# Reordering the attention handoffs of a recurrent-memory kernel: where q is turned, where scores start, how tAB is transposed and when vA leaves PSUM

## The chip, the cores and the metric

The kernel runs on one core of one Trainium2 chip. The metric is the device time of one execution in microseconds (us); smaller is better. The kernel before took 2384.8 us (median of three executions, 2383.08 to 2384.88).

## The reference, cut to what matters

Two independent branches read the same x (2048 rows of 1024, bf16) and are mixed by a gate. Branch A is a transformer layer that walks over 64 segments of 32 rows, one after the other: the first 8 rows of a segment's output are the memory rows that stand ahead of the next segment. Branch B is a feed-forward block without any recurrence.

```python
for s in range(n_seg):                      # 64 segments, one after the other
    xs = x[:, s * seg_len:(s + 1) * seg_len, :].copy()
    h = jnp.concatenate([mem, xs], axis=1)  # 8 memory rows + 32 rows
    q = jnp.einsum('btd,dhe->bhte', h, Wq)  # 32 heads of 128
    k = jnp.einsum('btd,dhe->bhte', h, Wk)
    v = jnp.einsum('btd,dhe->bhte', h, Wv)
    scores = jnp.einsum('bhqe,bhke->bhqk', q, k) * scale
    scores = jnp.where(mask[None, None], scores, -1000000000.0)
    p = _softmax(scores, axis=-1)
    o = jnp.einsum('bhqk,bhke->bhqe', p, v)
    o = jnp.einsum('bhte,hed->btd', o, Wo)
    mem = o[:, :M, :].copy()                # needed by the next segment
    outs.append(o[:, M:, :])
...
return g * a + (1 - g) * (_gelu(x @ w_gate) * (x @ w_up) @ w_down)
```

## The kernel before, in words

**Order.** The program is a list of operations, each with an engine, written in one order by hand; every engine runs its own operations strictly in that order, and a small planner (`_Prog`) adds semaphore waits from what each operation reads and writes. Two kinds of waits matter below. A PSUM bank is tracked as a whole: an operation waits for the last operation of every other engine on that bank. SBUF is tracked by address, and many tiles share addresses: `vA` lies on `oT` (and on the stage "o"), `pAB` on `kT`, `E8` and `tAB` on `qT` (which is also the stage "q"), and the stage "p" (`pS` in the profile) on `oRc` and `a_bf`.

**A step** is one segment. Its 32 heads are worked in two halves of 16 ("0" and "1" in the code; the trace's first and second attention of a step). The weights do not fit into SBUF: each of Wq, Wk, Wv, Wo is cut into pieces of 128 x 2048 (512 KB), 8 for each half. 50 slots hold them; 14 of the slots are shared by a piece of either half, so that each step reloads 14 pieces (2 of k, 2 of q, 4 of v, 6 of o) as soon as the first half has used them. A q, k or v piece is 4 matmuls of 512 columns that run beside each other in four column groups. The order of pieces in a step (`HEAD` and `BODY`, L322) is: k0 0-3, q0 0-1, the previous step's o1 4-7, q0 2-3, v0 0-3, k0 4-7, q0 4-7, v0 4-7; then k1, q1, o0 (in four groups of two pieces), v1, and o1 0-3. `on(m, r, n, ...)` in `plan` (L848) hangs other work ahead of the n-th piece of matrix m and half r.

**From projections to attention.** A projection leaves its bank through ScalarE into a stage (`evac`, L614), TensorE turns it by four 128 x 128 transposes (`turn`, L631) and VectorE copies it out (`trans`, L617). `scores` (L644) does the mask and score matmuls into bank SS, then VectorE and ScalarE do the softmax, up to a 128 x 512 32-block transpose into `tAB` (L672). `attend` (L674) multiplies by `vA` (L681) and by `vB` (L686, the second 256 columns of `tAB`) into the banks B0, B1, B2 and SS; `take` copies the four banks into `oT`; `rest_o` (GpSimd, L702) saves eight columns.

**Around the change.** In a step s > 0 the first half's q is turned ahead of v0's piece 6 through bank TT, its scores run ahead of k1's piece 0, `vA` is evicted (ScalarE) ahead of q1's piece 3, which is after k1's eviction into `pS` (ahead of q1's piece 1); the attention runs ahead of o0. Then k1 and q1 are turned through TT, and the second half's scores run ahead of o0's last group (6).

**Step boundary.** The output sum of two halves sits in bank XO; `fold(s, 0)` (VectorE, L763 and L764) adds its first half into `a_bf`, `next_mem` (L773, L776) turns it into the next step's memory columns, and k0 of the next step can begin. TensorE does f2's pieces or `warm` (L799) matmuls meanwhile. `fold(s, 1)` follows ahead of q0's piece 2, and a GpSimd DMA (L938) saves `a_bf` to `a_scr`.

**Fills.** The memory-free part of the projections (the last 8 rows of each segment) is made for four segments at a time (`fill`, L789): one or two such units a step up to step 58, `FILL` (L832): (k,1) and (q,1) when s % 4 is 0; (v,0) and (q,0) when 1; (v,1) when 2; (k,0) when 3. The first unit is evicted by `fill_evac` into the stage "k", and if it is k or q it is turned (`fill_put`, L816: TensorE, VectorE L821, and a GpSimd DMA into `qk_scr`, L824) ahead of o1's piece 2. The second (always q) is put out of the stage "o" ahead of the next step's v0 piece 2.

After the 64 steps come the remaining output rows (L960) and branch B (from L971), which the change does not touch.

Of the kernel before, what the change touches and what calls it, by code (L numbers as in the profile page):

```python
# [191 lines left out]
class _V:  # L192
# [11 lines left out]
    r = _T.r  # L204
# [6 lines left out]
def bass_gated_mix__memory_aug_recurrent_mem_tr__geglu_ffn__prompt_kernel(  # L211
# [34 lines left out]
    with ExitStack() as es:  # L246
# [380 lines left out]

        def turn(st):
            def f(e):
                for j in range(4):  # L630
                    ins = e.transpose(PBV[TT][:, j * 128:(j + 1) * 128], st[:, j * 128:(j + 1) * 128], ident[:, :])  # L631
                return ins
            op("pe", f, rd=[st.r(), ident.r()], wr=[BK(TT)])

        def trans(to, st):
            turn(stage[st])
            dve_copy(to[:, :, :, 0:32].rearrange("p j g c -> p (j g) c"),
                     PBV[TT][:, 0:512].rearrange("p (j g c) -> p (j g) c", g=4, c=32), [BK(TT)], [to.r()])

# [4 lines left out]
        def scores(u):  # L644

            def f(e):
# [24 lines left out]
               rd=[E8.r(), st8.r(8, 16)], wr=[pAB.r(256)])  # L671
            op("dve", lambda e: e.transpose(tAB[:, :], pAB[:, 0:512]), rd=[pAB.r()], wr=[tAB.r()], after=[fin])  # L672

        def attend(u, by=((2, "act"), (3, "dve"), (0, "act"), (1, "dve"))):  # L674
            bo = (B0, B1, B2, SS)

            def f(e):
                for j in range(4):
                    for g in range(4):
                        r = slice(32 * g, 32 * g + 32)  # L680
                        e.matmul(PB[bo[g]][:, j * LQ:(j + 1) * LQ], lhsT=vA[r, j, :],  # L681
                                 rhs=tAB[r, 64 * j:64 * j + LQ],
                                 start=(j == 0), stop=False, skip_group_check=True)
                for g in range(4):
                    r = slice(32 * g, 32 * g + 32)
                    ins = e.matmul(PB[bo[g]][:, 0:4 * LQ].rearrange("p (j c) -> p j c", j=4)[:, :, 24:40], lhsT=vB[r, u, :],  # L686
                                   rhs=tAB[r, 256:512].rearrange("p (j x) -> p j x", j=4)[:, :, 24:40],
                                   start=False, stop=True, skip_group_check=True)
                return ins
            op("pe", f, rd=[vA.r(), tAB.r(), vB.r()], wr=[BK(b) for b in bo])  # L690
            take(by)
            if len(by) == 4:
                rest_o(u)

        def take(by):
            n = 4 * LQ
            for g, eng in by:
                b = (B0, B1, B2, SS)[g]
                cp[eng](oT[:, g, :, :].rearrange("p j c -> p (j c)"), PB[b][:, 0:n], [BK(b)], [oT.r(g * n, (g + 1) * n)])
# [115 lines left out]

        def fill_put(m, u, G, st):  # L816
            if m == "v":
                return
            st = stage[st]
            turn(st)  # L820
            op("dve", lambda e: e.tensor_copy(st[:, :].rearrange("p (i x c) -> p x i c", i=4, x=16),  # L821
                                              PBV[TT][:, 0:512].rearrange("p (x i c) -> p x i c", x=16, i=4)), rd=[BK(TT)], wr=[st.r()])
            m4 = 3 * u if m == "q" else 1 + u
# [16 lines left out]
        def some(fs, n):  # L840
            return lambda: run(fs, n)
# [6 lines left out]
        def plan(s):  # L848
# [37 lines left out]
            on("v", 0, 4, lambda: put_rest())  # L886
            on("v", 0, 6, lambda: trans(qT, "q"))
            if s == 0:
                on("k", 1, 0, lambda: load_v(0, slice(0, 1)))
            on(*(("k", 1, 1) if s == 0 else ("q", 1, 3)), lambda: evac(bank_of["v", 0], vA, "act"))  # L890
            on("k", 1, 1 if s == 0 else 0, lambda: scores(ua))
            if s == 0:
                on("k", 1, 1, lambda: attend(ua))
                on("k", 1, 1, lambda: fill0("k", 1, B0, "k"))
# [6 lines left out]
            if s > 0:  # L901
                on("o", 0, 0, lambda: attend(ua, ((0, "dve"), (1, "dve"))))
            on("o", 0, 0, lambda: trans(kT, "p" if s else "k"))
            on("o", 0, 0, lambda: put_rest())
            on("o", 0, 0, lambda: evac(bank_of["q", 1], stage["q"], "act"))
            if s > 0:
                on("o", 0, 0, lambda: take(((2, "dve"), (3, "dve"))))
                on("o", 0, 0, lambda: rest_o(ua))
            on("o", 0, 2, lambda: trans(qT, "q"))
            on("o", 0, 6, lambda: scores(ub))  # L910
            on("v", 1, 0, some(f1, 3))
# [4 lines left out]
            if fl:  # L916
                on("o", 1, 0, lambda: fill_evac(*fl[0], A1, "k"))
                on("o", 1, 2, lambda: fill_put(*fl[0], "k"))
            if not last:
# [7 lines left out]
            nx = dict(s=s + 1)  # L927
            on("k", 0, 0, lambda: fold(s, 0), **nx)
            on("k", 0, 0, some(f2, 4) if two else lambda: warm(5), **nx)
            on("k", 0, 0, lambda: next_mem(s, 0), **nx)  # L930
            on("k", 0, 0, some(f2, 4) if two else lambda: warm(2), **nx)
            if two:
# [175 lines left out]
```

## Time and profile before

| | |
|---|---|
| median of three executions | 2384.8 us (2383.08 to 2384.88) |
| the profiled execution's own time | 2371.4 us |
| its span, first to last instruction | 2369.6 us |
| granted TensorE clock, mean | 0.983 |
| the 64 steps, first to last `fold(s, 0)` | 121.8 to 1724.3 us |
| mean step, 50 steps from 446.9 to 1697.0 us | 25.0 us |
| busy: TensorE matmul, VectorE, ScalarE, GpSimd | 2130.4, 1044.7, 519.1, 432.9 us |

The profile is one execution. Engines are PE (TensorE matmul), PEld (its weight loads), DVE (VectorE), ACT (ScalarE), POOL (GpSimd) and SP (SyncE, which issues most DMAs). L617 is line 617 of the kernel. In a timeline row stand the start in us, the time, the engine, the line, the operation, output<-inputs, how many were merged, and in brackets how long the engine had idled and what ended that. In the rows of the waits stand: engine, line, who was waited for, then us in total, number of times, the longest. A profiled execution is 13.4 us shorter than the median of the others, so a difference worked out from it is put on the median.

### The profile page before, as it was taken

Reading aid. Unit: us, or ns where it says so; the run is one execution under the profiler, and the core shown is the slowest. Engines: PE = TensorE matmul, PEld = TensorE weight load, DVE = VectorE, ACT = ScalarE, POOL = GpSimd, SP = SyncE. Lnnn points to the kernel's source line nnn. Section 1 sums busy time; section 2 is a strip of 40 time slices with the busy share of each in tenths; the row PEclk is TensorE's granted clock in tenths of the full one; section 3 lists DMA queues with packets and bytes.
Section 4 is the critical chain, followed back from the end, with each engine's and each line's share of the span. In section 5 each row is a group of like instructions: output and inputs, shape, how many; then the busy total and the mean of one; then the engine's idle time right before and its main releaser. Section 6 shows DMA issues by size and latency. Waiting matters only on the chain.

```text
span 2369.6 us, 74769 instructions
## 1 busy us (share of the span) xinstructions
PE 2130.4 (90%) x33827; PEld 1054.9 (45%) x33852; DVE 1044.7 (44%) x2438; ACT 519.1 (22%) x985; POOL 432.9 (18%) x821
## 2 busy tenths in 40 slices
PE   4588888989999998999899989988899999999999
PEld 2244444444444444444444444444464444444444
DVE  3344444444444444444444444444415436264463
ACT  1122222222222222222222222222103213032130
POOL 4322222222222222212222222222100000000000
PEclk9799999999999999999999999999999999999999
DMA  9979999989999999999899989999976260713530
GB/s 374 349 267 315 326 321 329 333 309 320 322 316 322 319 323 314 324 324 322 307 321 326 312 318 326 323 318 330 336 249 200 76 217 10 249 53 101 174 99 18
DMA packets 261453, 639.42 MB, mean 270 GB/s; under 512 B 28264, under 2 KB 102760, under 8 KB 261136
## 3 DMA queue, kind: packets, MB, share of 16 engines
q1 hardware_dynamic: 237312, 597.66, 72.4%
q0 software_dynamic: 13888, 26.31, 3.5%
q10 hardware_dynamic: 9936, 10.69, 1.3%
q8 instruction: 266, 4.36, 0.7%
q14 instruction: 51, 0.42, 0.0%
HBM read 596.85 MB, written 37.68 MB: 268 GB/s over the span
## 4 chain that ended last, share of the span: by engine, by line
PE 48%; DMA 29%; DVE 8%; issue 7%; ACT 5%; POOL 3%; ACTq 0%; SPq 0%; POOLq 0%
DMA a_scr<-a_bf 16%; PE pb L1009 14%; DMA wall<-wo_scr 6%; PE pb L719 6%; PE pb L1063 6%; PE pb L735 5%; PE pb L752 3%; PE pb L789 3%; DMA wall<-in_A_Wo_dram 2%; PE pb L960 2%; PE pb L1044 2%; PE pb L631 2%; PE pb L799 2%; ACT pS L614 1%; DMA xr_scr<-xr 1%
## 5 line engine op out<-in xcount | busy, mean ns | idle before, releaser
L719 PE MATMUL pb<-sl,hT 128*32 128x512 bf16 x12288 | 770.1, 382 | 7.2 <-issue 5.0
L719 PEld LDWEIGHTS pb<-sl,hT 128*32 128x32 bf16 x12288 | 342.4, 97 | 273.7 <-DVE hT L776 21.7
L789 PE MATMUL pb<-sl,hR 128*32 128x512 bf16 x3072 | 224.0, 393 | 9.2 <-issue 8.3
L1009 PE MATMUL pb<-xT,wg 128*128 128x512 bf16 x896 | 211.7, 379 | 0.7
L1009 PE MATMUL pb<-xT,wu 128*128 128x512 bf16 x896 | 211.7, 379 | 0.0
L752 PE MATMUL pb<-wall,oT 128*32 128x256 bf16 x4048 | 152.1, 276 | 38.0 <-DMA wall<-wo_scr 16.5
L763 DVE COPY part<-pb 64x256 f32<-64x256 f32 x128 | 54.0, 422 | 265.9 <-PE pb L752 263.4
L735 PE MATMUL pb<-wall,oT 128*32 128x512 bf16 x2048 | 153.1, 396 | 7.6 <-issue 0.2
L614 ACT ACTIVATE kS<-pb 128x512 bf16<-128x512 f32 x127 | 75.8, 597 | 367.9 <-PE pb L719 349.2
L617 DVE CAST oT<-pb 128x160 bf16<-128x160 f32 x382 | 105.5, 318 | 110.3 <-PE pb L686 110.3
L702 POOL COPY oRc<-oT 128x128 bf16<-128x128 bf16 x128 | 96.2, 752 | 313.3 <-DVE oT L617 311.9
L661 ACT ACTIVATE E<-pb 128x320 bf16<-128x320 f32 x128 | 56.0, 437 | 428.1 <-DVE pb L660 428.1
L1063 PE MATMUL pb<-wd,GT 128*128 128x512 bf16 x657 | 144.9, 379 | 2.1 <-DMA wd<-in_B_w_down_dram 1.2
L752 PEld LDWEIGHTS pb<-wall,oT 128*32 128x32 bf16 x4048 | 97.7, 97 | 93.8 <-issue 36.8
L1009 PEld LDWEIGHTS pb<-xT,wg 128*128 128x128 bf16 x896 | 87.0, 98 | 108.1 <-DVE GT L1025 3.7
L1017 ACT ACTIVATE s<-pb 128x512 f32<-128x512 f32 x112 | 66.7, 596 | 311.6 <-PE pb L1009 311.6
L1009 PEld LDWEIGHTS pb<-xT,wu 128*128 128x128 bf16 x896 | 87.5, 98 | 105.9
L1018 DVE SCALAR_TENSOR_TENSOR tp<-s,pb 128x512 f32<-128x512 f32 x112 | 77.0, 687 | 124.1 <-ACT s L1017 123.9
L659 DVE TENSOR_REDUCE st<-pb 128x8 f32<-128x320 f32 x128 | 62.9, 492 | 137.5 <-PE pb L653 137.5
L617 DVE COPY kT<-pb 128x512 bf16<-128x512 bf16 x128 | 53.7, 420 | 156.6 <-PE pb L631 156.6
L828 POOL COPY kT<-qkr 128x128 bf16<-128x128 bf16 x128 | 37.3, 291 | 451.6 <-DVE kT L617 389.3
L789 PEld LDWEIGHTS pb<-sl,hR 128*32 128x32 bf16 x3072 | 84.7, 99 | 68.6 <-issue 20.9
(93 smaller groups left out, 2249.9 us busy)
## 6 DMA issues: line engine op xcount, KB each, us to landing
wall<-wo_scr SPq DMA_DIRECT2D x336, 512.0 KB, 6.9
sl<-in_A_Wv_dram SPq DMA_DIRECT2D x268, 512.0 KB, 10.8
sl<-in_A_Wk_dram SPq DMA_DIRECT2D x142, 512.0 KB, 5.7
sl<-in_A_Wq_dram SPq DMA_DIRECT2D x142, 512.0 KB, 8.4
wd<-in_B_w_down_dram SPq DMA_DIRECT2D x42, 1024.0 KB, 5.5
wall<-in_A_Wo_dram SPq DMA_DIRECT2D x52, 512.0 KB, 7.9
wdF<-in_B_w_down_dram SPq DMA_DIRECT2D x7, 1024.0 KB, 7.7
wo_scr<-wall SPq DMA_DIRECT2D x12, 512.0 KB, 11.9
```

Source lines behind the costliest of these rows:

```text
L614: op("act", lambda e: e.activation(o, i, ACTF.Copy), rd=rd, wr=wr)
L617: op("dve", lambda e: e.tensor_copy(o, i), rd=rd, wr=wr)
L659: op("dve", lambda e: e.tensor_reduce(nm, sS, AX.X, ALU.max, negate=True), rd=[BK(SS)], wr=[st8.r(0, 8)])
L702: op("pool", lambda e: e.tensor_copy(oRc[:, :, 16 * u:16 * u + 16].rearrange("p c x -> p x c"), oT[:, :, :, 32:40].rearrange("p g j c -> p ...
L719: ins = e.matmul(PB[bk][32 * g:32 * g + 32, :], lhsT=h[:, i, :], rhs=w[:, g * 512:(g + 1) * 512], start=(n == 0), stop=(n == 7))
L735: ins = e.matmul(PB[XO][32 * g:32 * g + 32, :], lhsT=oT[:, j, x, 0:32], rhs=wall[:, na:nb + 1:nb - na, c:c + 256], start=(n == 0 and hp == 0),
L752: ins = e.matmul(PB[XO][32 * g:32 * g + 32, 256 * b:256 * b + 256], lhsT=oT[:, j, x, 0:32], rhs=w[:, c:c + 256], start=False, stop=(n % 4 ...
L789: ins = e.matmul(PB[b][32 * g:32 * g + 32, :], lhsT=h[:, k[2], :], rhs=w[:, g * 512:(g + 1) * 512], start=(n == 0), stop=(n == 7))
L1009: ins = e.matmul(PB[bk][:, 0:FB], lhsT=w[:, kc, cc:cc + 128], rhs=xT[:, :, :, kc, :].rearrange("p t i c -> p (t i) c"), start=(kc == 0), s ...
L1017: op("act", lambda e, hg=hg: e.activation(s1[:, :], hg, ACTF.Square, scale=SQ), rd=[BK(bg)], wr=[s1.r()])
L1018: op("dve", lambda e, hg=hg, t=t: e.scalar_tensor_tensor(out=t[:, :], in0=s1[:, :], scalar=1.0, in1=hg, op0=ALU.add, op1=ALU.mult), rd=[BK ...
L1063: ins = e.matmul(PB[bank[2 * k + hf]][:, :], lhsT=GT[:, j, tb * 128:(tb + 1) * 128], rhs=w[:, jj, hf * 512:(hf + 1) * 512], start=(j == 0) ...
```

## The change

Five edits, for the steps s > 0 unless said otherwise. (1) The first half's q is turned ahead of v0's piece 5 instead of 6, through bank A0 instead of TT, and its scores run ahead of v0's piece 7 instead of k1's piece 0. (2) `vA` of the first half is evicted ahead of k1's piece 4, which in ScalarE's order is now ahead of `pS`; the first attention's fourth bank is A0 instead of SS. (3) Of the first attention's four copies, VectorE does the first and the last and ScalarE the two between; the second half's q is turned through SS; the second half's scores run ahead of o0's group 4 instead of 6 (the title of the change counts pieces: a group is two). (4) `tAB` is transposed in two halves of 256 columns, and `attend` is two operations, the first of which needs the first half only (both attentions, all steps). (5) The first fill is evicted into the stage "q" instead of "k"; if it is k or q, its turn is done through SS right after `fold(s, 0)` at the step boundary, and its VectorE copy and its DMA after `next_mem(s, 0)`, instead of ahead of o1's piece 2.

```diff
--- before.py
+++ after.py
@@ -625,17 +625,17 @@
             else:
                 cp[how](t[:, :], PB[bank][:, :], [BK(bank)], [t.r()])
 
-        def turn(st):
+        def turn(st, bank=TT):
             def f(e):
                 for j in range(4):
-                    ins = e.transpose(PBV[TT][:, j * 128:(j + 1) * 128], st[:, j * 128:(j + 1) * 128], ident[:, :])
+                    ins = e.transpose(PBV[bank][:, j * 128:(j + 1) * 128], st[:, j * 128:(j + 1) * 128], ident[:, :])
                 return ins
-            op("pe", f, rd=[st.r(), ident.r()], wr=[BK(TT)])
-
-        def trans(to, st):
-            turn(stage[st])
+            op("pe", f, rd=[st.r(), ident.r()], wr=[BK(bank)])
+
+        def trans(to, st, bank=TT):
+            turn(stage[st], bank)
             dve_copy(to[:, :, :, 0:32].rearrange("p j g c -> p (j g) c"),
-                     PBV[TT][:, 0:512].rearrange("p (j g c) -> p (j g) c", g=4, c=32), [BK(TT)], [to.r()])
+                     PBV[bank][:, 0:512].rearrange("p (j g c) -> p (j g) c", g=4, c=32), [BK(bank)], [to.r()])
 
         sS = PB[SS][:, 0:320].rearrange("p (a c) -> p a c", a=8)
         nm, sm = st8[:, 0, :], st8[:, 1, :]
@@ -669,33 +669,38 @@
                 in0=E8[:, :, 32:40].rearrange("p (j c) k -> p j c k", c=2),
                 in1=sm.rearrange("p (j c) -> p j c", c=2).unsqueeze(3).to_broadcast([128, 4, 2, 8]), op=ALU.mult),
                rd=[E8.r(), st8.r(8, 16)], wr=[pAB.r(256)])
-            op("dve", lambda e: e.transpose(tAB[:, :], pAB[:, 0:512]), rd=[pAB.r()], wr=[tAB.r()], after=[fin])
-
-        def attend(u, by=((2, "act"), (3, "dve"), (0, "act"), (1, "dve"))):
-            bo = (B0, B1, B2, SS)
+            for c in (0, 256):
+                op("dve", lambda e, c=c: e.transpose(tAB[:, c:c + 256], pAB[:, c:c + 256]), rd=[pAB.r(c, c + 256)], wr=[tAB.r(c, c + 256)], after=[fin])
+
+        def attend(u, by=((2, "act"), (3, "dve"), (0, "act"), (1, "dve")), b3=SS):
+            bo = (B0, B1, B2, b3)
 
             def f(e):
                 for j in range(4):
                     for g in range(4):
                         r = slice(32 * g, 32 * g + 32)
-                        e.matmul(PB[bo[g]][:, j * LQ:(j + 1) * LQ], lhsT=vA[r, j, :],
-                                 rhs=tAB[r, 64 * j:64 * j + LQ],
-                                 start=(j == 0), stop=False, skip_group_check=True)
+                        ins = e.matmul(PB[bo[g]][:, j * LQ:(j + 1) * LQ], lhsT=vA[r, j, :],
+                                       rhs=tAB[r, 64 * j:64 * j + LQ],
+                                       start=(j == 0), stop=False, skip_group_check=True)
+                return ins
+
+            def f2(e):
                 for g in range(4):
                     r = slice(32 * g, 32 * g + 32)
                     ins = e.matmul(PB[bo[g]][:, 0:4 * LQ].rearrange("p (j c) -> p j c", j=4)[:, :, 24:40], lhsT=vB[r, u, :],
                                    rhs=tAB[r, 256:512].rearrange("p (j x) -> p j x", j=4)[:, :, 24:40],
                                    start=False, stop=True, skip_group_check=True)
                 return ins
-            op("pe", f, rd=[vA.r(), tAB.r(), vB.r()], wr=[BK(b) for b in bo])
+            op("pe", f, rd=[vA.r(), tAB.r(0, 256)], wr=[BK(b) for b in bo])
+            op("pe", f2, rd=[tAB.r(256), vB.r()], wr=[BK(b) for b in bo])
             take(by)
             if len(by) == 4:
                 rest_o(u)
 
-        def take(by):
+        def take(by, b3=SS):
             n = 4 * LQ
             for g, eng in by:
-                b = (B0, B1, B2, SS)[g]
+                b = (B0, B1, B2, b3)[g]
                 cp[eng](oT[:, g, :, :].rearrange("p j c -> p (j c)"), PB[b][:, 0:n], [BK(b)], [oT.r(g * n, (g + 1) * n)])
 
         def rest_o(u):
@@ -813,13 +818,19 @@
             else:
                 act_copy(st[:, :], PB[b][:, :], [BK(b)], [st.r()])
 
-        def fill_put(m, u, G, st):
+        def fill_turn(m, st, bank=TT):
+            if m != "v":
+                turn(stage[st], bank)
+
+        def fill_put(m, u, G, st, bank=None):
             if m == "v":
                 return
             st = stage[st]
-            turn(st)
+            if bank is None:
+                bank = TT
+                turn(st)
             op("dve", lambda e: e.tensor_copy(st[:, :].rearrange("p (i x c) -> p x i c", i=4, x=16),
-                                              PBV[TT][:, 0:512].rearrange("p (x i c) -> p x i c", x=16, i=4)), rd=[BK(TT)], wr=[st.r()])
+                                              PBV[bank][:, 0:512].rearrange("p (x i c) -> p x i c", x=16, i=4)), rd=[BK(bank)], wr=[st.r()])
             m4 = 3 * u if m == "q" else 1 + u
             op("pool", lambda e: e.dma_start(qk_scr[:, 4 * G:4 * G + 4, m4, :], st[:, :].rearrange("p (i y) -> p i y", i=4)),
                rd=[st.r()], wr=[("D", "qk", G, m, u)], lane="fq")
@@ -884,12 +895,14 @@
             if s == 0:
                 on("v", 0, 4, lambda: load_qk(0, 0))
             on("v", 0, 4, lambda: put_rest())
-            on("v", 0, 6, lambda: trans(qT, "q"))
+            on("v", 0, 5 if s else 6, lambda: trans(qT, "q", A0 if s else TT))
+            if s > 0:
+                on("v", 0, 7, lambda: scores(ua))
             if s == 0:
                 on("k", 1, 0, lambda: load_v(0, slice(0, 1)))
-            on(*(("k", 1, 1) if s == 0 else ("q", 1, 3)), lambda: evac(bank_of["v", 0], vA, "act"))
-            on("k", 1, 1 if s == 0 else 0, lambda: scores(ua))
+            on("k", 1, 1 if s == 0 else 4, lambda: evac(bank_of["v", 0], vA, "act"))
             if s == 0:
+                on("k", 1, 1, lambda: scores(ua))
                 on("k", 1, 1, lambda: attend(ua))
                 on("k", 1, 1, lambda: fill0("k", 1, B0, "k"))
                 on("q", 1, 0, lambda: fill0("q", 1, B1, "q"))
@@ -899,23 +912,28 @@
                 on("v", 0, 5, lambda: load_qk(s, 1))
             on(*(("q", 1, 1) if s else ("o", 0, 0)), lambda: evac(bank_of["k", 1], stage["p" if s else "k"], "act"))
             if s > 0:
-                on("o", 0, 0, lambda: attend(ua, ((0, "dve"), (1, "dve"))))
-            on("o", 0, 0, lambda: trans(kT, "p" if s else "k"))
-            on("o", 0, 0, lambda: put_rest())
-            on("o", 0, 0, lambda: evac(bank_of["q", 1], stage["q"], "act"))
-            if s > 0:
-                on("o", 0, 0, lambda: take(((2, "dve"), (3, "dve"))))
-                on("o", 0, 0, lambda: rest_o(ua))
-            on("o", 0, 2, lambda: trans(qT, "q"))
-            on("o", 0, 6, lambda: scores(ub))
+                on("o", 0, 0, lambda: attend(ua, ((0, "dve"),), A0))
+                on("o", 0, 0, lambda: evac(bank_of["q", 1], stage["q"], "act"))
+                on("o", 0, 0, lambda: trans(kT, "p"))
+                on("o", 0, 0, lambda: put_rest())
+                on("o", 0, 0, lambda: take(((1, "act"), (2, "act")), A0))
+                on("o", 0, 2, lambda: trans(qT, "q", SS))
+                on("o", 0, 2, lambda: take(((3, "dve"),), A0))
+                on("o", 0, 2, lambda: rest_o(ua))
+                on("o", 0, 4, lambda: scores(ub))
+            else:
+                on("o", 0, 0, lambda: trans(kT, "k"))
+                on("o", 0, 0, lambda: put_rest())
+                on("o", 0, 0, lambda: evac(bank_of["q", 1], stage["q"], "act"))
+                on("o", 0, 2, lambda: trans(qT, "q"))
+                on("o", 0, 6, lambda: scores(ub))
             on("v", 1, 0, some(f1, 3))
             on("o", 1, 0, lambda: evac(bank_of["v", 1], vA, "act"))
             on("o", 1, 0, some(f1, 3))
             on("o", 1, 0, lambda: attend(ub))
             on("o", 1, 0, some(f1, 8))
             if fl:
-                on("o", 1, 0, lambda: fill_evac(*fl[0], A1, "k"))
-                on("o", 1, 2, lambda: fill_put(*fl[0], "k"))
+                on("o", 1, 0, lambda: fill_evac(*fl[0], A1, "q"))
             if not last:
                 on("o", 1, 0, lambda: load_qk(s + 1, 0, "sp"))
             on("o", 1, 0, lambda: op("sp", lambda e: e.dma_start(o_scr[s], oRc[:, :, :].rearrange("p c x -> p (c x)")),
@@ -926,8 +944,12 @@
                 return
             nx = dict(s=s + 1)
             on("k", 0, 0, lambda: fold(s, 0), **nx)
+            if fl:
+                on("k", 0, 0, lambda: fill_turn(fl[0][0], "q", SS), **nx)
             on("k", 0, 0, some(f2, 4) if two else lambda: warm(5), **nx)
             on("k", 0, 0, lambda: next_mem(s, 0), **nx)
+            if fl:
+                on("k", 0, 0, lambda: fill_put(*fl[0], "q", SS), **nx)
             on("k", 0, 0, some(f2, 4) if two else lambda: warm(2), **nx)
             if two:
                 on("q", 0, 2, lambda: fill_evac(*fl[1], B0, "o"), **nx)
```

## The prediction, as it was put on record

> **What bounds the kernel now.** I read the 40 slices first, then the busy table of a stretch in the 64 steps, then the waits, then the timeline of single steps.
>
> ```profile
> DMA  9979999989999999999899989999976260713530
> ```
>
> The 64 steps (121.8 to 1724.3 us) fill slices 2 to 29. There the DMA engines are over 0.9 busy all the time, and so is PE:
>
> ```profile
> 1000.00:1200.00 200.00, 181.23 (x3780) 91.47 (x3773) 91.83 (x246) 44.84 (x89) 48.20 (x97) 1.00 0.91 316
> ```
>
> In 200 us, 181.23 us are PE's and the DMA share is 0.91. Two resources are near their end, and neither is full: what is left is waits in a chain. Summing PE's idle time by the lines on its two sides, over 49 steps, gives 2.3 us of a 25.0 us step: 0.77 ahead of the first attention, 0.30 ahead of the second, 0.36 between Wo pieces of o1 (they wait for their weights), and 0.08 ahead of the fill's turn. The waits name the causes:
>
> ```profile
> ACT pS L614 <- DMA a_scr<-a_bf: 95.4, 61, 3.6
> PEld pb L681 <- ACT vA L614: 129.6, 123, 3.4
> PE pb L681 <- DVE tAB L672: 24.8, 51, 1.7
> ```
>
> `pS` lies on `a_bf`, so in 61 of 63 steps k1's eviction waits until the store of `a_bf` has landed; `vA` stands behind it on ACT, and the first attention behind `vA`. One such step:
>
> ```profile
> 1012.55 0.60 ACT L614 ACTIVATE pS<-pb 128x512 bf16<-128x512 f32 x1 [1.15 <-DMA a_scr<-a_bf]
> 1012.78 0.71 DVE L672 STREAM_TRANSPOSE tAB<-pAB 128x512 bf16<-128x512 bf16 x1
> 1013.04 0.59 ACT L614 ACTIVATE vA<-pb 128x512 bf16<-128x512 f32 x1
> 1013.69 0.27 PE L681 MATMUL pb<-tAB,vA 32*128 32x40 bf16 x16 [0.17 <-ACT vA L614]
> ```
>
> Landing, `pS`, `vA` 0.49 behind it, attention 0.65 behind that. The second attention mostly waits for the whole `tAB`; the fill's turn waits for its eviction:
>
> ```profile
> 1122.77 0.28 PE L681 MATMUL pb<-tAB,vA 32*128 32x40 bf16 x16 [0.36 <-DVE tAB L672]
> ...
> 1124.33 0.40 PE L631 MATMUL pb<-ident,kS 128*128 128x128 bf16 x4 [0.20 <-ACT kS L614]
> ```
>
> **The change, part by part.** Each gain is worked out in 49 steps (447 to 1697 us) from the start and end times in the trace.
>
> *First attention (edits 1, 2, 4).* `vA` moves into the time in which ACT waits for the landing. In steps with s % 4 of 1 and 2 its tile also waits for the store of the stage "o", which mostly lands 0.3 to 0.9 us ahead of `a_scr`; `pS` then slips by 0.15 at most. The new bank A0 makes the attention wait for `pS` itself: 0.65 after its start instead of 1.14 (queued behind on PE: k1's turn and o0). Turning q a piece earlier costs PE nothing as I read it: today its transposes start 0.29 us after ACT's end, and 0.05 behind ACT is possible (a fill's turn); a piece takes 0.21 (64 matmuls in 3.65 us), so they start 0.21 sooner with one piece less ahead of them. Scores and `tAB` come 0.21 sooner, the first half of `tAB` 0.33 more (half of 0.71); the second half 0.05 later than the whole would (an estimate for one more instruction; bounds 0 and 0.2, the shortest DVE rows, and DVE then idles, so either end costs little). With the new start as the latest of q1's last matmul, `pS` + 0.06 and half of `tAB`, and with the `vB` part waiting for the second half, the gain is 0.31 to 0.43 by kind of step, **mean 0.38**.
>
> *Second attention (edits 3, 4).* From the first attention to the second scores it is 2.71 us in 43 of 49 steps, though `qT` is out 0.37 earlier (1015.96 against 1016.39 in the step at 1000 us): o0's group 6 stands between. That goes, and `tAB`'s half gives another 0.33; then `vA`'s eviction after v1 is late next. Gain 0.28. ACT's two copies (0.25 each, behind q's 0.60) end before their Wo groups are due, and the last VectorE copy 0.6 before its own. In 8 or so steps of 49 the `qkr` load for the score's memory columns lands too late to use it all; I take off 0.02: **0.26**.
>
> *Fill's turn (edit 5), in two steps of four.* It takes 0.33 (four transposes) plus the 0.20 wait out of o1 and puts 0.33 behind `fold`. `fold` takes 0.97 to `next_mem`; f2's four pieces cover 0.85 of it, `warm(5)` 1.06. So `next_mem` comes 0.05 later in the one kind and 0.30 in the other. Net (0.48 + 0.23) / 4 = **0.18** a step. VectorE's copy (0.42) and the store move behind `next_mem`, where DVE and POOL idle.
>
> Were PE the only bound: 0.38 + 0.26 + 0.18 = 0.82 a step, 52 us over 63 steps.
>
> *What the DMAs take back.* The third of the six reloaded Wo pieces is what o1's last piece ahead of `fold` needs. In 24 of 47 steps that piece starts 0.13 to 0.14 us after the landing: there the step's end hangs on the DMA and nothing gained between o0 and o1 counts. The Wo reloads begin when o0 has used its pieces, so the first attention's gain moves them, unless the queue is still full: in 22 of 49 steps the first Wo piece lands only 1.41 to 1.47 after the last Wv piece, the closest seen, and moves by nothing. Taking for each step the later of PE's new arrival and the third landing so moved, the 0.82 becomes 0.45, less 0.09 for `next_mem` in the two kinds, and 0.02 for `qkr`: 0.34 a step, **21 us**.
>
> *The new store.* It leaves from the stage "q", which the next step's first q eviction overwrites. The store is issued about 2.2 us after `fold` starts in one of the two kinds (copy of `next_mem` at 1.40 + 0.30, then 0.42) and 1.9 in the other; the eviction is due at 7.7 and 8.5. So 5.45 and 6.6 us are allowed. The rows on its two sides:
>
> ```profile
> qk_scr<-kS POOLq DMA_DIRECT2D x31, 128.0 KB, 3.8
> qk_scr<-oS POOLq DMA_DIRECT2D x31, 128.0 KB, 7.3
> a_scr<-a_bf POOLq DMA_DIRECT2D x64, 64.0 KB, 7.0
> vB<-v_scr POOLq DMA_DIRECT2D x63, 64.0 KB, 6.9
> ```
>
> The same store today, issued around `fold`, takes 3.8 (the DMA share there falls to 0.2 to 0.6); those issued 5 us later, behind the Wk, Wq and Wv loads, 6.9 to 7.3. At 2 us it has one or two Wk loads beside it, which themselves land a median 5.7 after issue: I take 4.8, halfway, no wait. Bounds 3.8 (nothing) and 7.3 (below). Behind a late eviction stand, on ACT, the softmax's exponential, `vA` and `pS`, and on PE q's turn and everything after it.
>
> The Trainium skill bears on this bound: in "DMA: Bandwidth & Descriptors", Queues, rings and completion order, each DMA engine goes round-robin between the queues that have work, so a POOL store need not stand behind SP's loads. By that rule the bound would stay near 3.8. The trace doesn't show that: `vB`, a smaller transfer, takes 6.9 with four loads pending, and I keep the 7.3.
>
> **The rivals.**
>
> *PE is the bound after all:* the Wo landings move with everything else, and most of the 52 us arrives: 33 (if only the back-to-back queue gives way, 0.52 a step) to 52, some 2340. For it: DMA share 0.91, with some 1.5 us idle around each `fold`. Against it: the 24 steps at 0.13.
>
> *The DMAs take nearly all:* the Wo reloads stay back to back with the Wv loads in every step and never come sooner. The same working with those landings left where they are gives 0.27 a step (PE's own slack in the steps not at 0.13), less 0.09 and 0.02: 0.17, 11 us, 2374. If landings also slip as the queues fill, it goes towards nothing. For it: steps 60 to 62 have no fills, so that PE idles 1.6 us ahead of each second attention, and yet they take 23.3 to 24.5 us, with DMA busy 21.7 to 22.6. Against it: 0.4 to 1.2 us of idle DMA time a step after the first attention.
>
> *Slower, by the store from stage "q":* with latency L the two kinds lose (L - 5.45) + (L - 6.6) in four steps; at 6.7 us this eats the 4 x 0.34, and from there the kernel is slower. At 7.3, 0.64 a step is lost, 40 us, against 21 won: 2404. The wait would show ahead of the first q's turn, and in ACT's row for `qS`. For it: the 6.9 and 7.3 rows. Against it: these rows' issues come 3 to 5 us later, with more loads pending.
>
> *It doesn't do what it says:* ACT's eviction holds q's turn, so scores come no sooner, and the two half transposes cost as much as they give. The `vA` order alone stays: in the steps with the landing last, 0.49 less the same share to the DMAs, some 0.2 a step, 13 us, 2372.
>
> **How the numbers follow.** The profiled execution took 2371.4 us (span 2369.6), the median of the runs 2384.8; 21 us off either gives 2350.4 and **2364**. Chances: forecast (2352 to 2372) 0.47; PE bound (2332 to 2352) 0.17; DMAs (2372 to 2385) 0.17; slower by the store 0.13; not what it says 0.06. A measurement of this kernel tells some 0.2%, 4.8 us, from no change. Faster by more: 0.47 + 0.17, 0.10 of the DMA case and 0.04 of the last, 0.78; within 0.2%: the rest of these two and 0.01 of the store's, 0.10; slower: 0.12. The range 2338 to 2389 leaves out a third of the PE case's end and the slower case's upper part.
>
> **What would show it.** Right: `pS` <- `a_scr` stays, and PE's wait for `vA` ahead of the first attention shrinks from 0.77 to some 0.3 a step; first attention 0.65 after `pS`; second scores 2.3 after the first attention; the wait for `wall` in o1 grows from 0.36 to some 0.7; the DMA share rises from 0.91 to about 0.92 or 0.93; mean step 24.7. Wrong: ACT's `qS` waiting for `qk_scr<-qS`; q's first turn with PE idle ahead of it; a step as long as now with longer `wall` waits; a step of 24.2, with none.

## The result, and the profile after

The changed kernel is slower: 2389.8 us (median of 20 executions, 2378.5 to 2402.1) against 2375.4 us for the kernel before (20 executions, 2366.1 to 2386.5), a ratio of 1.0056 with a 95% interval of 1.0039 to 1.0073. The three executions shown ahead of the prediction (2383.1 to 2384.9) lie at the upper end of the range of the kernel before. So the 13.4 us between them and its profiled execution are chance, as far as these runs tell, and no property of profiled executions: the changed kernel's profiled execution took 2397.8 us, 8 us more than its median. The spans of the two profiled executions, 2396.0 and 2369.6 us, lie 26 us apart, nearly twice the medians' 14; the sums below are theirs, the verdicts are the medians'.

The busy row of the stretch that was read before hardly differs (181.23 of PE and a DMA share of 0.91 then):

```profile
1000.00:1200.00 200.00, 181.07 (x3778) 91.06 (x3782) 88.26 (x245) 47.39 (x106) 47.64 (x95) 0.98 0.90 315
```

The chain that ended last does. The lines of the kernel before, then of the changed one (L724 and L757 are the old L719 and L752):

```profile
DMA a_scr<-a_bf 16%; PE pb L1009 14%; DMA wall<-wo_scr 6%; PE pb L719 6%; PE pb L1063 6%; PE pb L735 5%; PE pb L752 3%; PE pb L789 3%; DMA wall<-in_A_Wo_dram 2%; PE pb L960 2%; PE pb L1044 2%; PE pb L631 2%; PE pb L799 2%; ACT pS L614 1%; DMA xr_scr<-xr 1%
```

```profile
PE pb L1031 14%; DMA wall<-wo_scr 13%; PE pb L724 12%; DMA qk_scr<-oS 7%; DMA qk_scr<-qS 6%; PE pb L1085 6%; PE pb L740 4%; PE pb L757 3%; PE pb L794 3%; PE pb L631 2%; PE pb L982 2%; PE pb L1066 2%; PE pb L804 2%; DMA a_scr<-a_bf 2%; DMA wall<-in_A_Wo_dram 2%
```

The store of `a_bf` has left the chain (16% to 2%). In its place stand the two stores into `qk_scr`, 13% together, and twice as much of the Wo reloads (`wall`). The waits of the changed kernel say who stood behind the stores (engine, line, waited for: us in total, times, longest):

```profile
ACT vA L614 <- DMA qk_scr<-oS: 66.4, 30, 4.2
...
PEld pb L682 <- ACT pS L614: 62.4, 47, 3.7
...
PE pb L757 <- DMA wall<-wo_scr: 40.1, 48, 2.3
...
POOL qk_scr L835 <- DMA qk_scr<-qS: 23.0, 13, 2.3
```

The last row has no counterpart in the steps of the kernel before and was in no part of the forecast: POOL, about to issue the second fill's store, waits until the *first* fill's store has landed. The row for `wall` was 16.5 us before.

Cutting the trace at each `fold(s, 0)` tells where a step got longer. Means of 46 steps (13 to 58), and by s % 4, which is called the kind of a step below:

| us | fold to first attention | to second | to next fold | step | s % 4 = 0 | 1 | 2 | 3 |
|---|---|---|---|---|---|---|---|---|
| before | 15.03 | 7.36 | 2.70 | 25.09 | 24.22 | 24.86 | 25.84 | 25.40 |
| changed | 15.48 | 7.38 | 2.66 | 25.52 | 25.60 | 27.08 | 24.99 | 24.32 |

Two kinds of step lose 1.38 and 2.22 us, two gain 0.85 and 1.08; (1.38 + 2.22 - 0.85 - 1.08) / 4 = 0.42 a step, 26 us over 63 steps. The kinds that lose are those whose previous step has a first fill of k: only its turn, copy and store were moved over the boundary, to the start of the next step. (These are means of one execution each, and kinds 2 and 3 come out shorter with edit 5 alone too, see e3.) One of the kind 0 (timeline of the changed kernel):

```profile
1547.28 0.78 POOL L835 DMA_DIRECT2D qk_scr<-qS  x1 [3.23 <-DVE qS L832]
...
1551.76 0.60 ACT L614 ACTIVATE kS<-pb 128x512 bf16<-128x512 f32 x1 [7.24 <-PE pb L724]
...
1555.50 0.60 ACT L614 ACTIVATE qS<-pb 128x512 bf16<-128x512 f32 x1 [3.14 <-DMA qk_scr<-qS]
1556.16 0.40 PE L631 MATMUL pb<-ident,qS 128*128 128x128 bf16 x4 [2.92 <-ACT qS L614]
```

The store goes out at 1547.28 and lands at 1555.1; the q eviction, which follows the k eviction by 0.87 us elsewhere, comes 3.74 us after it, and PE stands for 2.92 us. And one of the kind 1:

```profile
1470.06 0.77 POOL L835 DMA_DIRECT2D qk_scr<-qS  x1 [3.37 <-DVE qS L832]
...
1475.83 0.77 POOL L835 DMA_DIRECT2D qk_scr<-oS  x1 [1.70 <-DMA qk_scr<-qS]
...
1476.60 0.55 POOL L960 DMA_DIRECT2D a_scr<-a_bf  x1
...
1483.99 0.60 ACT L614 ACTIVATE vA<-pb 128x512 bf16<-128x512 f32 x1 [3.66 <-DMA qk_scr<-oS]
1484.48 0.59 ACT L614 ACTIVATE pS<-pb 128x512 bf16<-128x512 f32 x1
...
1485.13 0.27 PE L682 MATMUL pb<-tAB,vA 32*128 32x40 bf16 x16 [0.42 <-ACT pS L614]
```

Here the q eviction is not late. But both stores were given the lane "fq", and the planner lets a lane's next DMA wait for its last one. The second store leaves at 8.1 us after fold instead of 6.3, the store of `a_bf`, behind it on POOL, at 8.8 instead of 7.0; they land near 16 instead of 13.5 and 13.9 (medians of this kind), and `vA`, `pS` and the attention wait for both.

### The profile page after: what moved, and what is told of

Read it like the earlier page. It is cut to its first block, busy times and chain, and to the rows that moved or that the text cites. A ratio compares the mean times of both kernels' runs of the same rounds, so it can differ in the third digit from the quotient of the medians.

```text
span 2396.0 us, 74919 instructions
## 1 busy us (share of the span) xinstructions
PE 2158.5 (90%) x33852; PEld 1065.0 (44%) x33852; DVE 1026.2 (43%) x2440; ACT 543.8 (23%) x1111; POOL 434.3 (18%) x821
## 4 chain that ended last, share of the span: by engine, by line
PE 54%; DMA 34%; DVE 4%; issue 4%; ACT 3%; POOL 1%; ACTq 0%; SPq 0%; POOLq 0%
PE pb L1031 14%; DMA wall<-wo_scr 13%; PE pb L724 12%; DMA qk_scr<-oS 7%; DMA qk_scr<-qS 6%; PE pb L1085 6%; PE pb L740 4%; PE pb L757 3%; PE pb L794 3%; PE pb L631 2%; PE pb L982 2%; PE pb L1066 2%; PE pb L804 2%; DMA a_scr<-a_bf 2%; DMA wall<-in_A_Wo_dram 2%
## 5 line engine op out<-in xcount | busy, mean ns | idle before, releaser
L724 PE MATMUL pb<-sl,hT 128*32 128x512 bf16 x12288 | 774.4, 383 | 10.6 <-issue 9.9
L724 PEld LDWEIGHTS pb<-sl,hT 128*32 128x32 bf16 x12288 | 348.4, 97 | 288.4 <-issue 28.3
L757 PE MATMUL pb<-wall,oT 128*32 128x256 bf16 x4048 | 151.0, 276 | 58.4 <-DMA wall<-wo_scr 40.1
L740 PE MATMUL pb<-wall,oT 128*32 128x512 bf16 x2048 | 159.7, 406 | 10.3 <-issue 3.1
L757 PEld LDWEIGHTS pb<-wall,oT 128*32 128x32 bf16 x4048 | 98.4, 96 | 118.4 <-issue 62.6
L617 DVE CAST oT<-pb 128x160 bf16<-128x160 f32 x256 | 76.5, 320 | 131.4 <-PE pb L690 131.4
L614 ACT ACTIVATE qS<-pb 128x512 bf16<-128x512 f32 x189 | 112.9, 597 | 86.8 <-PE pb L690 45.7
L614 ACT ACTIVATE kS<-pb 128x512 bf16<-128x512 f32 x68 | 40.6, 597 | 387.9 <-PE pb L724 373.0
L614 ACT ACTIVATE vA<-pb 128x512 bf16<-128x512 f32 x128 | 76.2, 596 | 186.3 <-PE pb L724 119.9
```

The source lines that it names most:

```text
L614: op("act", lambda e: e.activation(o, i, ACTF.Copy), rd=rd, wr=wr)
L617: op("dve", lambda e: e.tensor_copy(o, i), rd=rd, wr=wr)
L724: ins = e.matmul(PB[bk][32 * g:32 * g + 32, :], lhsT=h[:, i, :], rhs=w[:, g * 512:(g + 1) * 512], start=(n == 0), stop=(n == 7))
L740: ins = e.matmul(PB[XO][32 * g:32 * g + 32, :], lhsT=oT[:, j, x, 0:32], rhs=wall[:, na:nb + 1:nb - na, c:c + 256], start=(n == 0 and hp == 0),
L757: ins = e.matmul(PB[XO][32 * g:32 * g + 32, 256 * b:256 * b + 256], lhsT=oT[:, j, x, 0:32], rhs=w[:, c:c + 256], start=False, stop=(n % 4 ...
```

## The experiments

Ratios are to the kernel before, with 95% intervals; 0.001 is 2.4 us. Theory STORE says that edit 5 is the whole loss, through these two waits; theory DMA, that the reordering crowds the weight queue.

**e1**, the changed kernel, the second store on a lane of its own:

```diff
-               rd=[st.r()], wr=[("D", "qk", G, m, u)], lane="fq")
+               rd=[st.r()], wr=[("D", "qk", G, m, u)], lane="fq" if bank == TT else "fs")
```

(The first fill's store has bank SS here and goes to "fs".)

> The changed kernel with one edit: the second fill's store (out of the stage "o") has a semaphore lane of its own instead of sharing that of the first fill's store. Theory STORE (the loss is edit 5: the store out of the stage "q" holds the next step's q eviction when s % 4 is 0, and through the shared lane holds the second fill's store and, behind it on POOL, the store of a_bf when s % 4 is 1): steps with s % 4 = 1 fall from 26.9 to about 24.4 us, those with 0 stay at 25.5; 2.4 / 4 x 63 = 38 us less than the changed kernel, ratio to the kernel before about 0.99. Theory DMA (the reordering crowds the DMA queues, the lane is no cause): steps with s % 4 = 1 stay near 26.9, ratio about 1.006.

Measured 0.9938 (0.9917 to 0.9959). How long POOL stood ahead of DMAs to or from `qk_scr` until the first fill's store had landed (us in total, times), in the kernel before, the changed kernel and e1; the one wait before and the one of e1 are from the start of the program, ahead of the steps:

```profile
  DMA qk_scr<-kS: 5.4, 1
```

```profile
  DMA qk_scr<-qS: 24.4, 14
```

```profile
  DMA qk_scr<-qS: 1.1, 1
```

The lane was worth 1.18%, 28 us (38 expected), and carries the change over the line between slower and faster. In the profile, steps of kind 1 fall from 27.08 to 25.70 (24.4 expected), and those of kind 0, for which no gain was expected, from 25.60 to 24.80: the store from the stage "q" lands there after a median 5.3 us instead of 6.9, and the q eviction's wait falls from a mean 1.42 us to 0.40. No second store leaves in these steps; why the first one lands sooner isn't shown.

**e2**, the changed kernel with edit 5 undone; edits 1 to 4 stay:

```diff
-                on("o", 1, 0, lambda: fill_evac(*fl[0], A1, "q"))
+                on("o", 1, 0, lambda: fill_evac(*fl[0], A1, "k"))
+                on("o", 1, 2, lambda: fill_put(*fl[0], "k"))
...
-                on("k", 0, 0, lambda: fill_turn(fl[0][0], "q", SS), **nx)
...
-                on("k", 0, 0, lambda: fill_put(*fl[0], "q", SS), **nx)
```

> The changed kernel with edit 5 undone (first fill evicted into the stage "k", turned and stored ahead of o1's piece 2, as before); edits 1 to 4 stay. Theory STORE: both waits go, every kind of step is shorter than before, by the 0.3 to 0.6 us that edits 1 to 4 were reckoned at (the 0.34 of the forecast, without the 0.09 that the turn costs at the boundary, and without the turn's own gain): 20 to 38 us, ratio 0.984 to 0.992. Theory DMA: edits 1 to 4 give nothing, ratio 1.000 to 1.006.

Measured 0.9891 (0.9859 to 0.9923), 2352.2 us: 26 us faster than before, as theory STORE has it. Not every kind is shorter, though: in the profile kind 0 takes 24.69 us (24.22 before), and the mean step 24.89 (25.09), which is half of what the medians say.

**e3**, the kernel before with edit 5 alone (the diff of e2 turned round, with the helpers that it needs).

> The kernel before with edit 5 alone (stage "q", turn through SS behind fold, copy and store behind next_mem). Theory STORE: all of the loss and none of the gain: steps with s % 4 = 0 about 1.4 to 2 us longer than before, those with 1 about 2 to 2.5 longer, 2 and 3 as before: some 0.9 x 63 = 55 us, ratio 1.015 to 1.025. Theory DMA: no loss without edits 1 to 4, ratio 0.997 to 1.002.

Measured 1.0122 (1.0088 to 1.0157): a loss without any of the other edits. Steps of kind 1 take 27.49 us (24.86 before), of kind 0 25.40 (24.22). The size is under the expected range; in the profile kinds 2 and 3, expected as before, take 25.13 and 24.86 us (25.84 and 25.40). So what these two kinds gained in the changed kernel can't be put down to edits 1 to 4 alone. Theory DMA falls.

**e12**, e3 with the own lane of e1.

> The kernel before with edit 5 and the own lane for the second fill's store (e3 with the edit of e1). What e3 lost by the lane goes; what stays is the wait of the next q eviction when s % 4 is 0, next_mem's later start, and the store's 128 KB in a stretch where the queues are full. Theory LANE FIRST (the shared lane is most of edit 5's loss): 22 to 28 us less than e3, ratio 1.000 to 1.004. Theory EVICTION FIRST (the q eviction's wait is most of it): ratio 1.006 to 1.011.

Measured 1.0053 (1.0033 to 1.0074), between the two ranges: the lane is 0.69%, 16 us, of edit 5's 1.22%, and 0.53% is something else.

**e4**, e1 with the boundary turn for the (k,1) fill alone; the (k,0) fill, whose store makes the q eviction wait, goes the old way (`if s % 4 == 3` at the three places of e2's diff).

> The changed kernel with the own lane of e1, and with the boundary turn kept for the (k,1) fill only (s % 4 = 0); the (k,0) fill (s % 4 = 3) goes back to the stage "k" ahead of o1's piece 2. Theory STORE: no wait of either kind is left (the (k,1) store lands near 7.5 us after fold and its q eviction is due at 8.7), so the kernel is as fast as e2 or up to 0.15 us a step faster: ratio 0.982 to 0.992. Theory DMA: ratio 1.000 to 1.006.

Measured 0.9935 (0.9909 to 0.9961): e1's value, with an interval that overlaps e2's a little. Taking that eviction's wait away, together with putting the turn back into o1, gained nothing that can be told; the wait alone, 0.40 us in one step of four, would be 6 us, about the size of the interval's half. This part of theory STORE isn't borne out.

**e13** and **e14**, e1 and e2 without the first fill's stores:

```diff
-                op(eng, lambda e: e.dma_start(qkr[:, u:u + 2, :], qk_scr[:, s, 2 * u:2 * u + 2, :]),
-                   rd=[("D", "qk", s // 4, m, u) for m in "qk"], ...
+                op(eng, lambda e: e.dma_start(qkr[:, u:u + 2, :], qk_scr[:, s % 4, 2 * u:2 * u + 2, :]),
+                   rd=[("D", "qk", 0, m, u) for m in "qk"], ...
...
+            if G > 0 and st is not stage["o"]:
+                return
             m4 = 3 * u if m == "q" else 1 + u
```

> e1 with the first fills' stores into qk_scr left out after the first four segments, and every segment loading the memory-free rows of the first four instead of its own (so scores are computed from stale rows); the fill's turn and copy stay at the step boundary. No store from the stage "q" is left, so neither the q eviction's wait nor its 128 KB behind fold. Theory STORE: what edit 5 still costs in e1 (0.47% against e2) is the store: e13 equals e14, both within 0.003 of 0.988. Theory TURN (the four transposes between fold and next_mem, which start the next step 0.25 us later): e13 stays 0.004 to 0.006 above e14.

> e2 with the same stores left out and the same stale rows loaded: the base for e13. The store leaves in the stretch around fold in which the DMA share is lowest, so leaving it out should be worth little: both theories expect the ratio of e2, 0.986 to 0.991.

Measured 0.9930 (0.9904 to 0.9956) and 0.9896 (0.9861 to 0.9932). Without the store e13 is where e1 was, so the store's bytes and the eviction's wait are not seen to cost anything in e1, within some 0.004; theory STORE, by which e13 equals e14, gets no support. The turn between `fold` and `next_mem` remains, but the 0.0034 between the two is under the 0.004 to 0.006 of theory TURN, and the intervals overlap: likely, not shown.

**e5**, the kernel before with `vA`'s eviction moved alone, and **e6**, with the halves of `tAB` alone:

```diff
-            on(*(("k", 1, 1) if s == 0 else ("q", 1, 3)), lambda: evac(bank_of["v", 0], vA, "act"))
+            on("k", 1, 1 if s == 0 else 4, lambda: evac(bank_of["v", 0], vA, "act"))
```

> The kernel before with one line moved: the first half's vA is evicted ahead of k1's piece 4 (ahead of pS on ScalarE) and nothing else; the first attention's fourth bank stays SS, so that it waits for vA and not for pS. Theory LANDING (the store of a_bf sets the first attention through ScalarE's order, and about half of a gain there survives the DMA queues): first attention earlier by 0.3 to 0.8 us in the median, 0.2 to 0.3 us a step left, ratio 0.992 to 0.995. Theory ELSEWHERE (the gain of e2 is edits 3 and 4): ratio 0.998 to 1.001.

> The kernel before with edit 4 alone (tAB transposed in halves, the attention in two operations). Theory LANDING: the first attention is held by vA and gains nothing; the second gains about 0.28 us, of which the wait for the third Wo piece takes most: 0.03 to 0.12 us a step, ratio 0.997 to 1.000. Theory ELSEWHERE: 0.3 us or more a step, ratio 0.992 or less.

Measured 0.9965 (0.9944 to 0.9987) and 0.9976 (0.9955 to 0.9998): 8 and 6 us, each a gain, e6's by a hair. e5 lies between the two ranges, e6 in that of LANDING.

**e7**, e2 with edit 3 undone too (the old block of lines at o0, with the bank A0).

> e2 with edit 3 undone too: the copies of the first attention, the second half's q turned through TT and the second scores ahead of o0's last group as in the kernel before; edits 1, 2 and 4 stay. Theory LANDING: the second scores lose 0.37 us, the halves still give 0.33, and the DMA queues would have taken most of it: 0 to 0.1 us a step worse than e2, ratio 0.988 to 0.993. Theory ELSEWHERE: most of e2's gain goes, ratio 0.996 to 1.000.

Measured 0.9937 (0.9916 to 0.9958). e5 and e6 add up to it (0.35% + 0.24% against 0.63%); edit 3 is worth the other 0.46% of e2, with intervals that just overlap: more than the 0 to 0.1 us a step expected, and e7 lies just outside LANDING's range.

**e8**, e2 with the store of `a_bf` issued right behind `fold(s, 1)`, ahead of the `vB` load; **e11**, e8 with `vA` behind `pS` in the kinds 1 and 2:

```diff
-            on("k", 0, 4, lambda: op("pool", lambda e: e.dma_start(a_scr[s]...
+            on("q", 0, 2, lambda: op("pool", lambda e: e.dma_start(a_scr[s]...
             on("q", 0, 2, lambda: load_v(s + 1), **nx)
```

```diff
-            on("k", 1, 1 if s == 0 else 4, lambda: evac(bank_of["v", 0], vA, "act"))
+            on(*(("q", 1, 2) if s % 4 in (1, 2) and 1 < s <= 58 else ("k", 1, 1 if s == 0 else 4)),
+               lambda: evac(bank_of["v", 0], vA, "act"))
```

> e2 with one line moved: the store of a_bf into a_scr is issued by POOL right behind fold of the second half, ahead of the vB load, instead of behind it and the second fill's store. Theory LANDING: it is issued 0.5 us (s % 4 of 0 and 3) to 1.5 us (1 and 2) sooner and lands as much sooner, pS and the first attention follow until vA or q1's matmuls are last: first attention 0.3 to 0.6 us sooner than in e2, 0.15 to 0.35 us a step, ratio 0.980 to 0.986. Theory ELSEWHERE (landings are set by the queue of weight loads, not by the issue): ratio as e2, 0.987 to 0.991.

> e8 with vA evicted behind pS again in the steps with s % 4 of 1 and 2, where vA's tile waits for the second fill's store (13.6 to 14.1 us after fold) while pS could leave at 12.2; the others keep vA first. Theory DMA SHARE: first attention of these kinds 0.5 to 0.7 us sooner than in e8, a third to a half of it left, over half of the steps: 5 to 11 us, ratio 0.985 to 0.990. If the weight queue takes all of it: ratio as e8, 0.988 to 0.992.

Measured 0.9901 (0.9869 to 0.9934) and 0.9890 (0.9860 to 0.9920): both as e2. So e8 is in ELSEWHERE's range, but not for its reason, and e11 in both of its ranges. The store did land 1.3 to 1.9 us sooner in every kind, and in e11 the first attention comes 14.31 us after fold (e2: 14.73, before: 15.03). The medians didn't follow: of the 0.42 us, 0.24 are gone by the second attention (the step of e11's profile is 0.26 shorter than e2's, which would be 16 us; the medians, 2350.0 and 2352.2, don't show them). A row that had 30.5 us in 6 waits before had grown in e2 already (174.6 in 32) and stands there in e11 too:

```profile
POOL kT L839 <- DMA qkr<-qk_scr: 173.3, 32, 6.7
```

This is the load of the second half's memory-free columns. The row is mostly idle time of GpSimd that costs nothing, and doesn't tell e11 from e2; what counts is how often GpSimd's copy of the columns into `kT` ends after VectorE's copy of q. Before, that is so in 3 of 46 steps, by 1.6 us in all; in e2 in 8, by 3.0; in e11 in 12, by 9.1. That is 0.13 us a step more than in e2, about half of the 0.24: for part of the steps the load is late for the sooner scores, and the rest is open.

**e9** and **e10**, the kernel before and e2 with two of the 14 weight reloads of a step left out, to relieve the weight queue:

```diff
         def fetch(n):
             k, t = uses[n][done[n]], slots[n]
+            if k[0] == "v" and k[2] in (1, 3) and done[n] > 0:
+                return
```

> The kernel before with two of the 14 weight reloads of each step left out (Wv pieces 1 and 3 keep whatever half was loaded first, so part of v is computed from the wrong weights); every instruction of the engines stays. It takes some 3 us of DMA time out of a step. It is the base for e10. With the DMA queues relieved, what is left are the waits in the engines' chain: from the shortest steps of each kind some 23.7 us a step, 80 us less, ratio about 0.965.

> e2 (edits 1 to 4) with the same two reloads left out. Theory DMA SHARE (edits 1 to 4 are worth about 0.75 us a step on the engines, and the weight queue takes back the rest): with the queue relieved the distance to e9 is 40 to 50 us, 0.017 to 0.021 of the kernel before, where e2 stands 0.011 off it. Theory SMALL GAIN (the engines gain no more than what e2 shows): the distance stays 20 to 28 us, 0.008 to 0.012.

Measured 0.9860 (0.9832 to 0.9888) and 0.9731 (0.9701 to 0.9761). The same stretch of e9, then of e10:

```profile
1000.00:1200.00 200.00, 182.42 (x3864) 93.21 (x3860) 93.23 (x251) 45.98 (x93) 49.34 (x98) 1.00 0.82 280
```

```profile
1000.00:1200.00 200.00, 187.18 (x3941) 96.15 (x3941) 93.33 (x256) 50.67 (x111) 49.81 (x100) 1.00 0.84 286
```

The DMA share fell from 0.91 to 0.82, and the kernel gained 33 us, not the 80 expected. Their distance is 0.0129 (31 us; each ratio's interval reaches 0.003 to either side) against e2's 0.0109: neither theory's range, nearer to SMALL GAIN. The third Wo piece speaks for the reason. From the issue of the first Wo reload to its landing it takes a median 7.70 us before, 7.77 in e2, 7.54 in e9 and 7.64 in e10, although in e9 the last Wv load lands 4.06 us ahead of the first Wo piece (1.58 before). And in e10 o1's last piece still starts within 0.2 us of that landing in 32 of 45 steps.

## Why the prediction was wrong, point by point

**The step that failed** is "The new store", with the sentence of edit 5 that the copy and the store move to where "DVE and POOL idle". It priced one wait, that of the stage's next writer, and put it at nothing; POOL's next store on the same lane was not looked at, though `lane="fq"` stands in the store's own line of the diff. Sharing the lane costs 28 us in the changed kernel (e1) and 16 us without edits 1 to 4 (e3 against e12). Without it the change would have been faster, 0.9938: 15 us where 21 were forecast.

**The store's latency** was taken as 4.8 us, between bounds of 3.8 and 7.3. The changed kernel's page has:

```profile
qk_scr<-qS POOLq DMA_DIRECT2D x31, 128.0 KB, 5.4
```

By kind the medians are 6.9 (s % 4 = 0, allowed 5.45) and 5.2 (s % 4 = 1, allowed 6.6). So the rival "Slower, by the store" had the right sign, place and row in the kind 0: q's eviction comes 9.51 us after fold where 7.83 (0.87 behind k's) was due. Its formula then gives (6.9 - 5.45) / 4 = 0.36 us a step, some 23 us, which the forecast's own 21 would nearly have paid for. For the kind 1, which loses most, it gives no wait at 5.2 us, and it doesn't know the lane. In e1 the eviction's wait is 0.40 us in the mean (4 of 11 steps), and e4 and e13 can't tell it from nothing. The Trainium skill's rule, that each DMA engine goes round-robin between the queues with work ("DMA: Bandwidth & Descriptors", Queues, rings and completion order), would have kept the store near 3.8; the measured 5.2 to 6.9 speak against using it so, and keeping the upper bound was right.

**The first attention** was right: `pS` + 0.65 in the median of e2, scores 0.22 sooner in the kind 1 (10.27 to 10.05; 0.21 forecast), 0.30 sooner in the mean for 0.38. **The second** too: scores 2.28 us after the first attention for the forecast 2.34 (2.71 before), and the shortest and usual distance of the attentions 6.86 for 7.18, 0.32; in the mean 0.21 for 0.26.

**What the DMAs take back** was about right in size and place and wrong in its reason. Edits 1 to 4 gain 26 us (18 to 34) in e2, of the 0.64 us a step, 40 us, that the forecast gave them with PE as the only bound. In the profile, from second attention to fold, e2 takes 3.01 us for 2.70, the 0.31 that stood against 0.51 won ahead of it; o1's last piece starts within 0.2 us of the third landing in 31 of 45 steps (23 before). But the forecast read "lands 1.41 to 1.47 after the last Wv piece" as a queue without a gap that holds the Wo reloads. e9 and e10 took two of the four Wv loads of a step away, and the third piece landed 0.13 to 0.16 us sooner after the burst's first issue than without that, no more.

**The fill's turn** was put at a gain of 0.18 a step, 11 us. e1 against e2 (0.9938, 0.9891) and e12 (1.0053) have edit 5 as a loss even without the lane. What of this is the turn stays open (e13, e14). The sum is also unclear: the 0.18 already holds `next_mem`'s 0.05 and 0.30, and the 0.26 the 0.02 for `qkr`, and the last step takes both off again; if the 0.45 was reached from the 0.82 as written, the sum is 0.45 us a step, 28 us.

**The rivals:** neither bound alone explains a loss, and e2 lies between them. "The DMAs take nearly all" left 11 us, under e2's 18 to 34; with PE as the only bound edits 1 to 4 would have given 40, above it. "It doesn't do what it says" is refuted by the first and second attention's numbers above.

## What to carry to other kernels

When a DMA is moved, look for three things besides the readers of what it writes: the next writer of its source, the next DMA that shares its completion semaphore, and whatever stands behind that DMA on the engine that issues it. The second showed in no step of the kernel before, because there the lane's last store had always landed, by 0.54 us or more, when the next went out; the one hint was the 5.4 us wait at the start of the program. Give two DMAs in flight two semaphores. The best version here is the changed kernel without edit 5 (e2, 2352.2 us, 0.9891); e8 and e11 can't be told from it.

## What the runs showed of the hardware that was not expected

A burst of six 512 KB reloads brings its third piece 7.5 to 7.8 us after the first issue (medians before and in e2, e9 and e10), whether the DMA share is 0.91 or 0.82, and whether the last Wv load lands 2.4 us after that issue (before) or 0.3 ahead of it (e9). The second piece did gain: 5.00 us in e9 for 6.04. Why the third doesn't follow isn't shown.

A share of 0.9, which the prediction read as over 0.9 all the time (its row of slices has 8s and 7s too), was taken for a resource near its end. Leaving out a seventh of a step's weight reloads gave 1.4% (e9), and the step's end still hangs on that burst in 32 of 45 steps of e10. The burst's own bytes may well set its time, as its pieces 3 to 6 land 1.3 to 1.5 us apart, before and in e9; no run made it smaller.
